# The activation and swish buffers of a fused attention and MoE kernel at other addresses relative to the weights

## The chip, the cores and the metric

One core of one Trainium2 chip. The metric is device time in microseconds for one execution; lower is better. Three runs of the kernel before took 1303.41, 1304.3 and 1307.11 us, median 1304.3 us.

## What is computed

Pooled attention, a dense swish MLP over its output, and a second MLP whose expert is chosen per token, all in float32 (N = 4608 tokens, d_model = 512):

```python
k_p = k.reshape(B, H, Sp, pool, D).mean(axis=3)          # pool = 8; v_p likewise
attn = softmax(scale * q @ k_p.T);  x = attn @ v_p       # 8 x 8 heads, 576 x 64
h = x @ w_in;  g = h * (1 / (1 + exp(-h)));  x = g @ w_out          # d_ff = 2048
...
e_idx = argmax(x @ w_gate);  do_compute = x @ w_skip > 0            # E = 8
h = maximum(x[mask] @ w1[e], 0);  y[mask] = gate_w * (h @ w2[e])    # F = 1024
out = x;  out[do_compute] += y
```

## The kernel before

**Products in three terms.** Each float32 operand of the large products is held as a high part (rounded to the matmul's float32r type) and a low part (the remainder); each product is high x high, high x low and low x high, three matmuls into one PSUM accumulator.

**The dense part** runs over 18 chunks of 256 tokens. Per chunk, attention leaves xh and xl, [128, 4, 256] words each: ScalarE copies the high part (`xh_copy`), VectorE subtracts (`xl_sub`). Then, for each of 16 blocks f of the hidden width:

- `mm1` (L320 to L328): 12 matmuls, four steps kk of three lines. L325 loads w_hi and streams xh (256 columns), L326 loads w_hi and streams xl, L327 loads w_lo and streams xh. The weight block is 128 columns, 512 bytes of a partition.
- tanh on ScalarE, `swish_t` on VectorE, then `swish_hi` (L340, ScalarE: gh) and `swish_lo` (L345, GpSimd or VectorE: gl), [128, 256] words each.
- `mm2` (L350 to L360): 6 matmuls, two token halves t of three lines. Here the activation is loaded and the weight streamed, 512 columns: L358 loads gh and streams v_hi, L359 loads gh and streams v_lo, L360 loads gl and streams v_hi.

**The order** on every engine comes from a list scheduler (`schedule`) that ranks steps by a table of costs and bonuses when the program is built; it knows how many buffers each kind has, not where they lie.

**The expert part** runs over pairs of token tiles sorted by expert: `xm1p` (L1055 to L1057) has mm1's shape with xh and xl from the same two buffers and the expert's weights in w_hi and w_lo; `xm2` (L1094 to L1096) loads hTh and hTl, which lie in v_hi, and streams weights that lie in w_hi and w_lo, 512 columns. Blocks of a single tile go through `single` (L1066 to L1068 for the first product).

**Addresses.** Pools lie one behind another in each partition's memory in the order in which they are opened, buffers of a pool behind one another. A weight block starts at its tile's start plus a multiple of 512 bytes, xh and xl blocks at their buffer's start plus a multiple of 1024, a half of gh or gl at its buffer's start or 512 behind it. So for each pair of operands the difference of their start addresses modulo 512 is one number per buffer. Start addresses modulo 512, worked out from the order and sizes of the tiles:

| tile | before | after |
|---|---|---|
| w_hi, w_lo, v_hi | 192 | 128 |
| v_lo | 384 | 448 |
| xh, first and second buffer | 256, 256 | 256, 320 |
| xl, first and second buffer | 256, 256 | 384, 416 |
| gh, three buffers | 256, 256, 256 | 416, 480, 0 |
| gl, three buffers | 256, 256, 256 | 0, 0, 0 |

Of the kernel before, what the change touches and what calls it, by code (L numbers as in the profile page):

```python
# [7 lines left out]
F32 = mybir.dt.float32  # L8
F32R = mybir.dt.float32r
BF16 = mybir.dt.bfloat16  # L10
I32 = mybir.dt.int32
# [13 lines left out]
KD = DM // 128  # L25
DFF = 2048
NF = DFF // 128
E = 8
# [3 lines left out]
NTILE = NT // 128  # L32
CH = 256
TPC = CH // 128
LAG = 3
PAIR = 256
NPX = NT // PAIR
NX = E + (NT - E) // PAIR
NXP = 28
# [13 lines left out]
def body(tc, const, q, k, v, w_in, w_out, w_skip, w_gate, w_r, w1, w2, out, x2d, lst, base, nch, nxt):  # L53
# [3 lines left out]
    with ExitStack() as ctx:  # L57
        def pool(name, bufs, **kw):
            return ctx.enter_context(tc.tile_pool(name=name, bufs=bufs, **kw))

        wp = pool("wp", 1)
        xt_p = pool("xt_p", 2)
        t_p = pool("t_p", 2)
        g_p = pool("g_p", 3)
        x2_p = pool("x2_p", 4)
        jk_p = pool("jk_p", 1)
        r_p = pool("r_p", 2)
# [7 lines left out]
        ident = const["ident"]  # L75
        triu = wp.tile([128, 128], BF16, name="triu")
        ones = wp.tile([128, 128], BF16, name="ones")
        rev = wp.tile([128, 1, E], F32, name="rev")
        ecap = wp.tile([128, 1, E], F32, name="ecap")
        tok = wp.tile([128, NTILE], F32, name="tok")  # L80
        skp = wp.tile([128, NTILE], F32, name="skp")
        wr = wp.tile([128, KD, E + 1], F32, name="wr")
# [3 lines left out]
        w4_hi = w_hi.rearrange("p f (k n) -> p f k n", n=128)  # L86
        w4_lo = w_lo.rearrange("p f (k n) -> p f k n", n=128)
        wb = wp.tile([128, (E + 1) * DM], F32, name="wb")
        pad = wp.tile([128, NTILE, 4], I32, name="pad")
        room = wp.tile([128, 6 * 512 + 6 * HP * 2 * SP], F32, name="room")  # L90
        lone = ExitStack()
        ctx.push(lone)
# [148 lines left out]
        q_t, P_t, PT_t, xh_t, xl_t = {}, {}, {}, {}, {}  # L241
# [64 lines left out]
        def x_parts(i):  # L306
            j, t = divmod(i, TPC)
            if t == 0 and j not in xh_t:
                xh_t[j] = xt_p.tile([128, KD, CH], F32R, tag="xh", name="xh")
                xl_t[j] = xt_p.tile([128, KD, CH], F32R, tag="xl", name="xl")  # L310
            return (x[j][:, :, t * 128:t * 128 + 128] for x in (xh_t, xl_t))

        def xh_copy(i):
# [24 lines left out]
            nc.vector.scalar_tensor_tensor(out=t, in0=t, scalar=1.0, in1=ps, op0=ALU.add, op1=ALU.mult)  # L338

        def swish_hi(j, f, t, ps):  # L340
            gh = g_p.tile([128, CH], F32R, tag="gh", name="gh")
            nc.scalar.copy(out=gh, in_=t)  # L342
            return j, f, t, gh

        def swish_lo(j, f, t, gh, eng=nc.vector):  # L345
            gl = g_p.tile([128, CH], F32R, tag="gl", name="gl")
            eng.tensor_tensor(out=gl, in0=t, in1=gh.bitcast(F32), op=ALU.subtract)  # L347
            g_t[j, f] = (gh, gl)

# [31 lines left out]
        sh = [128, TPC, E]  # L381

        def route_a(j):
            lg = lg_t[j]
            l = lg[:, :, 0:E]
            mx = r_p.tile([128, TPC, 1], F32, tag="rmx", name="rmx")
            m2 = r_p.tile([128, TPC, 1], F32, tag="rm2", name="rm2")
            cm = r_p.tile([128, TPC, 1], F32, tag="cm", name="cm")
            oh = r_p.tile(sh, F32, tag="oh", name="oh")
            ohb = r_p.tile(sh, BF16, tag="ohb", name="ohb")  # L390
            nc.vector.tensor_reduce(out=mx, in_=l, axis=AX.X, op=ALU.max)
            nc.vector.tensor_tensor(out=l, in0=l, in1=mx.to_broadcast(sh), op=ALU.subtract)
            nc.vector.scalar_tensor_tensor(out=oh, in0=l, scalar=0.0, in1=rev.to_broadcast(sh), op0=ALU.is_ge,
                                           op1=ALU.mult)
            nc.vector.tensor_reduce(out=m2, in_=oh, axis=AX.X, op=ALU.max)
            nc.vector.tensor_tensor(out=oh, in0=oh, in1=m2.to_broadcast(sh), op=ALU.is_equal)
            nc.vector.tensor_scalar(out=cm, in0=lg[:, :, E:E + 1], scalar1=0.0, scalar2=None, op0=ALU.is_gt)
            nc.vector.tensor_tensor(out=oh, in0=oh, in1=cm.to_broadcast(sh), op=ALU.mult)
            nc.vector.tensor_copy(out=ohb, in_=oh)
            rt[j] = (oh, ohb, cm)  # L400
# [10 lines left out]
            nc.scalar.activation(out=l, in_=l, func=ACTF.Exp)  # L411

        def route_gate(j):
            gw = r_p.tile([128, TPC, 1], F32, tag="gw", name="gw")
            nc.vector.tensor_reduce(out=gw, in_=lg_t.pop(j)[:, :, 0:E], axis=AX.X, op=ALU.add)
            nc.vector.tensor_scalar(out=gw, in0=gw, scalar1=1e-9, scalar2=None, op0=ALU.add)
            row = row_t[j] = r_p.tile([128, TPC, 4], I32, tag="row", name="row")
            nc.vector.reciprocal(out=row[:, :, 2:3].bitcast(F32), in_=gw)
            for t in range(TPC):
                i = TPC * j + t  # L420
                nc.vector.tensor_copy(out=row[:, t, 0:2], in_=tok[:, i:i + 1].to_broadcast([128, 2]))
            nc.vector.memset(row[:, :, 3:4], 0)

        def route_place(j):
            oh, ohb, cm = rt.pop(j)
            ps = rp_t.pop(j)
            ds = r_p.tile(sh, F32, tag="ds", name="ds")
            dd = r_p.tile([128, TPC, 1], F32, tag="dd", name="dd")
            du = du_t[j] = r_p.tile([128, TPC, 1], I32, tag="du", name="du")
            for t in range(TPC):  # L430
                nc.vector.tensor_tensor(out=ds[:, t], in0=ps[:, 0, t], in1=base, op=ALU.add)
                nc.vector.tensor_tensor(out=base, in0=base, in1=ps[:, 1, t], op=ALU.add)
            nc.vector.tensor_tensor(out=ds, in0=ds, in1=ecap.to_broadcast(sh), op=ALU.add)
            nc.vector.tensor_tensor(out=ds, in0=ds, in1=oh, op=ALU.mult)
            nc.vector.tensor_reduce(out=dd, in_=ds, axis=AX.X, op=ALU.add)
            i = TPC * j
            sk = skp[:, i:i + TPC].rearrange("p (t o) -> p t o", o=1)
            nc.vector.scalar_tensor_tensor(out=cm, in0=cm, scalar=0.0, in1=sk, op0=ALU.is_equal, op1=ALU.mult)
            nc.vector.tensor_tensor(out=du, in0=dd, in1=cm, op=ALU.add)
# [12 lines left out]
        def dense():  # L452
# [48 lines left out]
            def op(name, cost, fn, after=(), take=None, bonus=0.0, linger=0.0):  # L501
                bonus += bonus_of.get(name[0], {}).get(phase(*name), 0.0)
                ops[name] = (cost, fn, [a for a in after if a], take, bonus, linger)

            def put_in(key, v):
                st[key] = v
# [131 lines left out]

            tail = {(1, f): NF + f for f in range(NF - LAG, NF)}
            slot = {**tail, **{(j, f): j * NF + f for j in range(2, nch) for f in range(NF)}}  # L640
            at = {n: jf for jf, n in slot.items()}
            for j in range(nch):
                for f in range(NF):
                    n = slot.get((j, f), -1)

                    def back(name, k):
                        return n - k in at and (name, *at[n - k])
# [3 lines left out]
                       [("xl", TPC * j + t) for t in range(TPC)]  # L651
                       + [("lo", 2 * f), f > 0 and ("mm1", j, f - 1), (j, f) == (1, NF - LAG) and ("mm1", 0, NF - 1),
                          back("mm1", 1), back("sw", 2), back("mm2", LAG + 1)], [("h", ("h", j, f))])
                    op(("th", j, f), {"A": 0.27}, lambda e, j=j, f=f: put_in(("t", j, f), tanh(*st["h", j, f])),
# [164 lines left out]
        def flat(w, a, b):  # L819
            return w[:, a:b].rearrange("p f n -> p (f n)")  # L820
# [4 lines left out]
        W2h4, W2l4 = (w.rearrange("p (k n) -> p k n", n=DM) for w in (W2h, W2l))  # L825
        hTh, hTl = (flat(v_hi, a, a + 4).rearrange("p (k n) -> p k n", n=PAIR) for a in (8, 12))
        xg = [room[:, KD * F2 + a * 2 * DM:KD * F2 + (a + 1) * 2 * DM].rearrange("p (t n) -> p t n", n=DM)
# [3 lines left out]
        xT_t, own = {}, []  # L831
# [51 lines left out]
        def row_of(t):  # L883
            return t.rearrange("p e o -> p o e")

        def first_table():
# [8 lines left out]
            nc.vector.tensor_tensor(out=top, in0=key, in1=kmax.to_broadcast([1, E, 1]), op=ALU.is_equal)  # L895
            nc.vector.scalar_tensor_tensor(out=skip, in0=cnt0, scalar=float(PAIR), in1=top, op0=ALU.min, op1=ALU.mult)
            nc.vector.tensor_tensor(out=f2[:, 0:1], in0=row_of(top), in1=row_of(ie), op=ALU.mult)
# [6 lines left out]
        def table_iota():  # L904
            nc.gpsimd.iota(jt, pattern=[[0, 1], [PAIR, NPX]], base=0, channel_multiplier=0,
                           allow_small_or_imprecise_dtypes=True)
            nc.gpsimd.iota(it, pattern=[[1, NXP], [0, 1]], base=0, channel_multiplier=0,
                           allow_small_or_imprecise_dtypes=True)
            nc.gpsimd.iota(ib, pattern=[[PAIR, NXP], [0, 1]], base=0, channel_multiplier=0,
                           allow_small_or_imprecise_dtypes=True)  # L910
# [122 lines left out]

        def x_turn_hi(i, t, ps):
            if i < 2 and t == 0:
                xT_t[i] = [xt_p.tile([128, KD, PAIR], F32R, tag=tag, name=tag) for tag in ("xh", "xl")]
            nc.scalar.copy(out=xT_t[i % 2][0][:, :, t * 128:t * 128 + 128], in_=ps)

        def x_turn_lo(i, t, ps):
# [282 lines left out]
```

## Time and profile before

| | |
|---|---|
| median of three runs | 1304.3 us |
| profiled execution, its own time | 1307.36 us |
| its span, first to last instruction | 1305.6 us |
| TensorE (PE) busy | 1261.9 us, 97% |
| weight loads (PEld) busy | 1128.2 us, 86% |
| VectorE (DVE) / ScalarE (ACT) / GpSimd (POOL) busy | 809.0 / 557.4 / 458.3 us |
| mean granted TensorE clock | 0.997 of 2.4 GHz |

Busy time counts a matmul from its start to its modelled end, and matmuls overlap in the pipeline: a matmul shown with 282 ns may be followed by the next after 118 ns. So what a matmul costs when others stand behind it is read from the starts of neighbours in the timeline, and the busy share only says where TensorE is idle.

### The profile page before, as it was taken

The page shows a single profiled execution, that of the slowest core. Times are in us where ns is not written, and L with a number is a line of the kernel's source. Part 1 is how long each engine was busy: PE and PEld are TensorE (multiplying, and loading weights), DVE is VectorE, ACT ScalarE, POOL GpSimd, SP SyncE. Part 2 cuts the span into 40 slices and gives each one's busy share as a digit, 9 for nine tenths or more (in the row PEclk, how much of TensorE's full clock was granted, in tenths as well). Part 3 has the DMA queues.
Part 4 walks back from the last instruction along what each step waited for, and adds up shares of the span by engine and source line. Part 5 has one row for each costly group of instructions (what it writes and reads, how often), then busy time and mean ns, then how long its engine had stood idle before and what let it go on. Part 6 is the DMA issues. An engine that isn't in the chain of part 4 may idle for free. (4 is left out here: it accounts for less than half of the span.)

```text
span 1305.6 us, 24485 instructions
## 1 busy us (share of the span) xinstructions
PE 1261.9 (97%) x8508; PEld 1128.2 (86%) x8508; DVE 809.0 (62%) x2112; ACT 557.4 (43%) x1609; POOL 458.3 (35%) x552
## 2 busy tenths in 40 slices
PE   4899999999999999999999999999999999999986
PEld 3789889988989988889899989998998999989775
DVE  7998897576575584574675654744773222333777
ACT  4876543434434443434344444343341121223675
POOL 2312154344434333533534333332432112133654
PEclk9999999999999999999999999999999999999999
DMA  7655412101121121112110110000411111426770
GB/s 234 223 201 197 144 40 82 46 13 64 40 69 64 35 73 41 40 55 76 34 63 19 41 41 17 34 33 1 172 40 58 59 34 58 170 66 220 260 287 26
DMA packets 51152, 113.32 MB, mean 87 GB/s; under 512 B 12279, under 2 KB 13303, under 8 KB 50864
## 3 DMA queue, kind: packets, MB, share of 16 engines
q1 hardware_dynamic: 44960, 96.39, 21.7%
q0 software_dynamic: 6032, 14.97, 3.4%
q8 instruction: 80, 1.31, 0.4%
q14 instruction: 80, 0.66, 0.2%
HBM read 134.05 MB, written 26.62 MB: 123 GB/s over the span
## 5 line engine op out<-in xcount | busy, mean ns | idle before, releaser
L325 PE MATMUL psh<-xh,w_hi 128*128 128x256 f32 x1152 | 325.2, 282 | 1.0 <-DVE t L338 1.0
L326 PE MATMUL psh<-xl,w_hi 128*128 128x256 f32 x1152 | 323.1, 280 | 1.5 <-DVE xl L319 1.5
L327 PE MATMUL psh<-xh,w_lo 128*128 128x256 f32 x1152 | 322.2, 280 | 0.0
L347 POOL TENSOR_TENSOR gl<-t,gh 128x256 fp32r<-128x256 f32 x231 | 184.5, 800 | 344.8 <-ACT gh L342 230.5
L378 DVE SCALAR_TENSOR_TENSOR junk<-x,wb 128x512 bf16<-128x512 f32 x306 | 242.8, 793 | 21.7 <-ACT x L367 16.0
L338 DVE SCALAR_TENSOR_TENSOR t<-t,psh 128x256 f32<-128x256 f32 x288 | 119.5, 416 | 192.4 <-ACT t L332 190.4
L358 PE MATMUL pso<-v_hi,gh 128*128 128x512 f32 x576 | 230.3, 400 | 0.1
L332 ACT ACTIVATE t<-psh 128x256 f32<-128x256 f32 x288 | 110.8, 385 | 272.4 <-PE psh L327 248.6
L325 PEld LDWEIGHTS psh<-xh,w_hi 128*128 128x128 f32 x1152 | 216.9, 188 | 10.8 <-DVE t L338 1.5
L359 PE MATMUL pso<-v_lo,gh 128*128 128x512 f32 x576 | 226.1, 393 | 0.0
L360 PE MATMUL pso<-v_hi,gl 128*128 128x512 f32 x576 | 225.0, 391 | 0.3 <-POOL gl L347 0.3
L326 PEld LDWEIGHTS psh<-xl,w_hi 128*128 128x128 f32 x1152 | 216.9, 188 | 9.2 <-DVE xl L319 1.9
L327 PEld LDWEIGHTS psh<-xh,w_lo 128*128 128x128 f32 x1152 | 216.2, 188 | 0.0
L342 ACT CAST gh<-t 128x256 fp32r<-128x256 f32 x288 | 117.0, 408 | 150.8 <-DVE t L338 121.8
L360 PEld LDWEIGHTS pso<-v_hi,gl 128*128 128x128 f32 x576 | 108.1, 188 | 27.6 <-POOL gl L347 1.2
L358 PEld LDWEIGHTS pso<-v_hi,gh 128*128 128x128 f32 x576 | 108.0, 187 | 16.9 <-ACT gh L342 0.8
L359 PEld LDWEIGHTS pso<-v_lo,gh 128*128 128x128 f32 x576 | 108.4, 188 | 15.3
L1058 ACT ACTIVATE v_hi<-p 128x256 fp32r<-128x256 f32 x88 | 33.5, 384 | 179.0 <-PE p L1057 169.9
L1059 DVE SCALAR_TENSOR_TENSOR v_hi<-p,v_hi 128x256 fp32r<-128x256 f32 x88 | 36.9, 423 | 114.6 <-ACT v_hi L1058 103.1
L275 ACT ACTIVATE room<-pss,mx 128x72 f32<-128x72 f32 x288 | 88.1, 326 | 30.5 <-DVE mx L267 27.4
L1055 PE MATMUL p<-xh,w_hi 128*128 128x256 f32 x352 | 100.4, 285 | 0.0
L1057 PE MATMUL p<-xh,w_lo 128*128 128x256 f32 x352 | 98.3, 279 | 0.0
(189 smaller groups left out, 2118.3 us busy)
## 6 DMA issues: line engine op xcount, KB each, us to landing
more<-in_w_dram SPq DMA_DIRECT2D x72, 512.0 KB
room<-in_w_dram SPq DMA_DIRECT2D x40, 512.0 KB
wb<-in_w_dram SPq DMA_DIRECT2D x36, 512.0 KB
room<-in_k_dram SPq DMA_DIRECT2D x32, 288.0 KB
room<-in_v_dram SPq DMA_DIRECT2D x64, 144.0 KB
room<-in_q_dram SPq DMA_DIRECT2D x36, 256.0 KB
out_dram<-x SPq DMA_DIRECT2D x36, 256.0 KB
x2d<-x SPq DMA_DIRECT2D x36, 256.0 KB
```

The costliest lines, as they stand in the source:

```text
L325: nc.tensor.matmul(out=ps, lhsT=w4_hi[:, f, kk], rhs=xh[:, kk], start=(kk == 0), stop=False)
L326: nc.tensor.matmul(out=ps, lhsT=w4_hi[:, f, kk], rhs=xl[:, kk], start=False, stop=False)
L327: nc.tensor.matmul(out=ps, lhsT=w4_lo[:, f, kk], rhs=xh[:, kk], start=False, stop=(kk == KD - 1))
L332: nc.scalar.activation(out=t, in_=ps, func=ACTF.Tanh, scale=0.5)
L338: nc.vector.scalar_tensor_tensor(out=t, in0=t, scalar=1.0, in1=ps, op0=ALU.add, op1=ALU.mult)
L342: nc.scalar.copy(out=gh, in_=t)
L347: eng.tensor_tensor(out=gl, in0=t, in1=gh.bitcast(F32), op=ALU.subtract)
L358: nc.tensor.matmul(out=ps, lhsT=gh[:, ts], rhs=v_hi[:, f], start=(f == 0), stop=False)
L359: nc.tensor.matmul(out=ps, lhsT=gh[:, ts], rhs=v_lo[:, f], start=False, stop=False)
L360: nc.tensor.matmul(out=ps, lhsT=gl[:, ts], rhs=v_hi[:, f], start=False, stop=(f == NF - 1))
L378: nc.vector.scalar_tensor_tensor(out=junk, in0=x2_t[i], scalar=1.0, in1=wb[:, e * DM:e * DM + DM], op0=ALU.mult, op1=ALU.mult, accum_out=l ...
L1055: nc.tensor.matmul(out=ps, lhsT=W1h4[:, kk, m], rhs=xh[:, kk], start=(kk == 0), stop=False)
```

## The change

The two xh, two xl, three gh and three gl buffers get a pool of their own each, opened in the order of two tables; a number other than 0 in a table puts an unused tile of that many bytes ahead of the buffer. `rev`, `ecap` and `pad`, small tiles of the routing, move from the weights' pool to places between these buffers. Five small route tiles (rmx, rm2, gw, ds, dd) get one buffer instead of two. Chunk j uses buffer j % 2 of xh and xl as before, and the gh and gl buffers are used in turn as before. The instructions and their order on each engine stay the same.

```diff
+SPOTS_X = (("rev", 0), ("xh0", 64), ("xh1", 64), ("pad", 0), ("xl0", 0), ("xl1", 32))
+SPOTS_G = (("gh0", 0), ("gh1", 64), ("gh2", 32), ("gl0", 0), ("gl1", 0), ("gl2", 0))
...
-        xt_p = pool("xt_p", 2)
+        sep = [0]
+
+        def own_pool(name, gap):
+            if gap:
+                sep[0] += 1
+                pool(f"sep{sep[0]}", 1).tile([128, gap // 4], F32, name="sep")
+            return pool(name, 1)
+
+        x_p = {}
+        for n, gap in SPOTS_X:
+            if n == "rev":
+                x_p[n] = pool("rev_p", 1)
+            elif n == "pad":
+                x_p[n] = pool("pad_p", 1)
+            else:
+                x_p[n] = own_pool("p" + n, gap)
         t_p = pool("t_p", 2)
-        g_p = pool("g_p", 3)
+        g_ps = {n: own_pool("p" + n, gap) for n, gap in SPOTS_G}
+        turn = {"x": [], "gh": 0, "gl": 0}
+
+        def x_tiles(side):
+            for part in ("xh", "xl"):
+                n = f"{part}{side}"
+                yield x_p[n].tile([128, KD, CH], F32R, tag=n, name=part)
+
+        def g_tile(part):
+            n = turn[part]
+            turn[part] = n + 1
+            return g_ps[f"{part}{n % 3}"].tile([128, CH], F32R, tag=f"{part}{n % 3}", name=part)
...
-        rev = wp.tile([128, 1, E], F32, name="rev")
-        ecap = wp.tile([128, 1, E], F32, name="ecap")
...
-        pad = wp.tile([128, NTILE, 4], I32, name="pad")
+        pad = x_p["pad"].tile([128, NTILE, 4], I32, name="pad")
+        rev = x_p["rev"].tile([128, 1, E], F32, name="rev")
+        ecap = x_p["rev"].tile([128, 1, E], F32, name="ecap")
...
-                xh_t[j] = xt_p.tile([128, KD, CH], F32R, tag="xh", name="xh")
-                xl_t[j] = xt_p.tile([128, KD, CH], F32R, tag="xl", name="xl")
+                xh_t[j], xl_t[j] = x_tiles(j % 2)
...
-            gh = g_p.tile([128, CH], F32R, tag="gh", name="gh")
+            gh = g_tile("gh")
...
-            gl = g_p.tile([128, CH], F32R, tag="gl", name="gl")
+            gl = g_tile("gl")
...
-            ds = r_p.tile(sh, F32, tag="ds", name="ds")
-            dd = r_p.tile([128, TPC, 1], F32, tag="dd", name="dd")
+            ds = r_p.tile(sh, F32, tag="ds", name="ds", bufs=1)
+            dd = r_p.tile([128, TPC, 1], F32, tag="dd", name="dd", bufs=1)
...
-                xT_t[i] = [xt_p.tile([128, KD, PAIR], F32R, tag=tag, name=tag) for tag in ("xh", "xl")]
+                xT_t[i] = list(x_tiles(i))
```

## Rows read from the trace of the kernel before

**Rows 1.** The page: span, busy time of each engine, granted clock in tenths by slice.

```profile
span 1305.6 us, 24485 instructions
PE 1261.9 (97%) x8508; PEld 1128.2 (86%) x8508; DVE 809.0 (62%) x2112; ACT 557.4 (43%) x1609; POOL 458.3 (35%) x552
...
PEclk9999999999999999999999999999999999999999
```

**Rows 2.** Busy us (x instructions) by stretch: PE, PEld, DVE, ACT, POOL; clock, DMA share, GB/s.

```profile
0.00:60.00 60.00, 37.25 (x208) 30.91 (x208) 51.33 (x101) 38.17 (x116) 19.41 (x37) 1.00 0.68 225
60.00:200.00 140.00, 137.19 (x962) 122.77 (x961) 127.58 (x313) 85.23 (x256) 33.95 (x50) 1.00 0.43 146
200.00:1000.00 800.00, 798.09 (x5585) 718.57 (x5584) 491.94 (x1526) 327.88 (x1058) 307.00 (x396) 1.00 0.15 51
1000.00:1140.00 140.00, 140.00 (x927) 128.61 (x927) 37.95 (x74) 26.04 (x63) 24.46 (x24) 1.00 0.22 70
1140.00:1306.00 166.00, 149.40 (x835) 127.34 (x834) 100.23 (x102) 80.12 (x119) 73.52 (x45) 0.98 0.50 174
```

**Rows 3.** Groups by form on PE: shapes, xcount | busy us, mean ns | idle before.

```profile
L325 PE MATMUL psh<-xh,w_hi 128*128 128x256 f32 x1152 | 325.2, 282 | 1.0 <-DVE t L338 1.0
...
L327 PE MATMUL psh<-xh,w_lo 128*128 128x256 f32 x1152 | 322.2, 280 | 0.0
L358 PE MATMUL pso<-v_hi,gh 128*128 128x512 f32 x576 | 230.3, 400 | 0.1
L359 PE MATMUL pso<-v_lo,gh 128*128 128x512 f32 x576 | 226.1, 393 | 0.0
L360 PE MATMUL pso<-v_hi,gl 128*128 128x512 f32 x576 | 225.0, 391 | 0.3 <-POOL gl L347 0.3
L1055 PE MATMUL p<-xh,w_hi 128*128 128x256 f32 x352 | 100.4, 285 | 0.0
...
L1094 PE MATMUL py<-w_hi,v_hi 128*128 128x512 f32 x80 | 31.2, 390 | 0.0
```

**Rows 4.** Timeline of PE, mm2 then mm1: start us, us, line, operands.

```profile
399.75 0.40 PE L358 MATMUL pso<-v_hi,gh 128*128 128x512 f32 x1
399.99 0.39 PE L359 MATMUL pso<-v_lo,gh 128*128 128x512 f32 x1
400.22 0.40 PE L360 MATMUL pso<-v_hi,gl 128*128 128x512 f32 x1
400.45 0.40 PE L358 MATMUL pso<-v_hi,gh 128*128 128x512 f32 x1
400.69 0.39 PE L359 MATMUL pso<-v_lo,gh 128*128 128x512 f32 x1
400.92 0.39 PE L360 MATMUL pso<-v_hi,gl 128*128 128x512 f32 x1
401.15 0.28 PE L325 MATMUL psh<-xh,w_hi 128*128 128x256 f32 x1
...
403.97 0.40 PE L358 MATMUL pso<-v_hi,gh 128*128 128x512 f32 x1
```

**Rows 5.** Timeline of PEld, the weight loads, in the same stretch.

```profile
399.75 0.19 PEld L359 LDWEIGHTS pso<-v_lo,gh 128*128 128x128 f32 x1
...
401.15 0.19 PEld L326 LDWEIGHTS psh<-xl,w_hi 128*128 128x128 f32 x1
```

**Rows 6.** Timeline of PE, xm2 of one pair: its first matmul and what follows its 48.

```profile
1118.03 0.39 PE L1094 MATMUL py<-w_hi,v_hi 128*128 128x512 f32 x1
...
1128.93 0.28 PE L1055 MATMUL p<-xh,w_hi 128*128 128x256 f32 x1
```

**Rows 7.** Timeline of PE, the sixteen short matmuls of the last router sums.

```profile
967.16 1.85 PE L1122 MATMUL psl<-wr,x2T 128*128 128x9 f32 x16
968.86 0.36 PE L1055 MATMUL p<-xh,w_hi 128*128 128x256 f32 x1
```

**Rows 8.** Busy us (x instructions) of L325 alone between 60 and 200 us.

```profile
60.00:200.00 140.00, 47.92 (x170) 1.00 0.43 146
```

More of the change, by code (lines that the diff above doesn't have):

```diff
@@ L385, in route_a @@
             l = lg[:, :, 0:E]
-            mx = r_p.tile([128, TPC, 1], F32, tag="rmx", name="rmx")
-            m2 = r_p.tile([128, TPC, 1], F32, tag="rm2", name="rm2")
+            mx = r_p.tile([128, TPC, 1], F32, tag="rmx", name="rmx", bufs=1)
+            m2 = r_p.tile([128, TPC, 1], F32, tag="rm2", name="rm2", bufs=1)
             cm = r_p.tile([128, TPC, 1], F32, tag="cm", name="cm")
@@ L413, in route_gate @@
         def route_gate(j):
-            gw = r_p.tile([128, TPC, 1], F32, tag="gw", name="gw")
+            gw = r_p.tile([128, TPC, 1], F32, tag="gw", name="gw", bufs=1)
             nc.vector.tensor_reduce(out=gw, in_=lg_t.pop(j)[:, :, 0:E], axis=AX.X, op=ALU.add)
```

## The prediction

> **What bounds the kernel now.** I read the page first [rows 1]: TensorE is busy for 1261.9 of 1305.6 us (97%), VectorE for 62%, and the granted clock stands at its upper level, 2.4 GHz, in every slice. The table by stretches [rows 2] shows where the rest is: between 200 and 1000 us TensorE is idle for 1.9 us, between 1000 and 1140 us for none. So in those 940 us nothing but TensorE sets the time; it is idle for 22.8 us before 60 us and for 16.6 us after 1140 us. Between 60 and 200 us VectorE is busy for 127.6 of 140 us, so a faster TensorE would gain less there.
>
> The groups by form [rows 3] give the counts. mm1 issues its three lines together, 1152 matmuls of 256 columns on each, and xm1p its three, 352 on each: 4512 instructions of one shape. mm2 has three lines of 576 (512 columns); in xm2 the row of py stands for its shape. A busy matmul is not a matmul at its peak, so I take steps from start to start [rows 4]: from 401.15 to 403.97 us stand 24 matmuls of mm1, 117.5 ns each; the six of mm2 ahead of them take 1.40 us, 233.3 ns each. In xm2 [rows 6] 48 matmuls of 512 columns take 10.90 us, 227.1 ns each. The same work at the same clock: 6 ns apart.
>
> What differs is where the operands lie. Each matmul streams one operand while the stationary one of the next is loaded: the load of L359 starts in the same hundredth of a microsecond as the matmul of L358 [rows 4, 5]. For such a pair I take the start of the activation side less that of the weight side, modulo 512. Before, every pair of mm1 and xm1p has 64; in mm2 L358 and L360 (v_hi streams, gh is loaded) have 64, L359 (v_lo streams, gl is loaded) has 384; xm2 has 0. The mean durations [rows 3] follow in part: at 0, 390 ns (py); at 384, 393; at 64, 400 and 391, in the mean 395.5.
>
> **The change, part by part.** No instruction is added, removed or moved: every engine has the same rows in the same order. What moves is addresses. In mm1 and xm1p the pair goes from 64 to 128 or 192 (xh) and 256 or 288 (xl). In mm2 L358 and L360 go from 64 to 288, 352 or 384, in turn; L359 goes from 384 to 64; xm2 stays at 0.
>
> 1. mm1 and xm1p. No row has 256 columns at the new distances, so I bound the step. Below: 256 more columns cost 227.1 - 117.5 = 109.6 ns [rows 4, 6], so a step holds 7.9 ns that its columns don't need; without them, 4512 x 7.9 ns = 35.6 us less. The load alone doesn't stop this: the 16 short matmuls of L1122, each behind a load of 128 columns, step by (968.86 - 967.16)/16 = 106 ns [rows 7]. Above: the mean at 64 is 5.5 ns over that at 0; if the new distances cost that more than now, 4512 x 5.5 = 24.8 us. The nearest row to the new distances is L359's, at 384, which is 128 the other way round: 2.5 ns under the mean at 64. There is one weight load to a matmul in either shape, so I take the same 2.5 ns per matmul: 4512 x 2.5 = 11.3 us less.
> 2. mm2. L358 and L360 (1152 instructions) go from the mean at 64 to about 384: 1152 x 2.5 = 2.9 us less. L359 (576) goes the other way: 1.4 us more. Net 1.4 us less; at best all six step as in xm2, 1728 x (233.3 - 227.1) = 10.7 us less; at worst L358 and L360 keep theirs and L359 reaches L358's 400, 576 x 7 = 4.0 us more.
> 3. xm2 at nothing: its distance stays. The one-tile blocks at the end (L1066 to L1068) at nothing: they stand in the last stretch, where TensorE is idle for 16.6 us anyway [rows 2], and are few.
> 4. Five small route tiles lose their second buffer. Each is written and read by VectorE alone, in its own order, so no wait comes of it: nothing. Moving pad, rev and ecap, and the separators, costs no instruction.
>
> Of this the matmuls of mm1 between 60 and 200 us, three lines of 170 [rows 8], may lose their 510 x 2.5 ns = 1.3 us to VectorE; I leave that to the range. Sum: -11.3 - 1.4 = **-12.7 us**. The profiled execution took 1307.4 us and would take 1294.7; it lies 3.1 us above the median of the three runs, 1304.3, from which the sum gives 1291.6.
>
> Here a page speaks against the change. The rows show a matmul step that differs by 6 ns between mm2 and xm2 [rows 4, 6]. The Trainium skill, "TensorE: Matmul & The Clock Gate", Part 2, step 1, says that TensorE reads the streaming operand and the weights through two independent ports, and that loading the next weights takes no read bandwidth from the running matmul. By that the sum would be 0 and not -12.7 us. By that rule steps of one shape should be alike wherever the operands lie, and these traces show two that aren't.
>
> **The rivals.**
> - *Nothing to gain.* If the 117.5 ns of mm1 are the stream's and the load's own (106 ns for a load [rows 7] plus a hand-over), no distance matters for 4512 of the instructions, and mm2's two shifts nearly cancel: 1304. For it: L325 and L327, which load from different weight tiles, agree to 2 ns, and L360, at 64, takes 391, hardly more than xm2's 390 [rows 3], so the address may not be what tells L358 from L360. Against it: mm2 and xm2 differ. The page of the Trainium skill named above, "TensorE: Matmul & The Clock Gate", would give this case.
> - *The distances are worse.* The load takes 106 ns for its 512 bytes [rows 7], in which the stream of mm1 reads its 1024 bytes; so the stream gains 512 bytes on the load and passes it once, modulo 512. Where depends on the distance: at 0 at the very ends of the load (xm2, 390 ns), at 64 in mm1 after seven eighths of it; in L359 at three quarters (393 ns), in L358 at one eighth (400 ns). If a passing in the midst costs more than one near the end, the change moves all 4512 to between seven sixteenths and three quarters: with L359's excess over xm2, 3 ns, 4512 x 3 = 13.5 us more, 1318. It decides from the point at which xl0 and xl1, the middle ones, make L326 step longer than L325 and L327. For it: 0 is the best distance in the trace and the change leaves it further behind. Against it: L360 sits at the place of L358 and pays 1 ns.
> - *It doesn't do what it says*: the addresses follow from the order and sizes of the tiles, so I give that no chance of its own.
>
> **How the numbers follow.** A fewer-stalls case gets 0.48, nothing to gain 0.22, worse distances 0.30. About 0.3% (3.9 us) is what a measurement of this kernel can tell from no change; the first case lies beyond it from 0.9 ns per matmul of mm1 on, the third likewise, so the chances are those of the cases. The predicted time is the first case's, 1292 us (the sum, rounded up). The ends of the unknown costs are 1304.3 - 35.6 - 10.7 = 1258 and 1304.3 + 24.8 + 4.0 = 1333; both ask that every buffer hit its extreme, and the distances differ from buffer to buffer. 1268 to 1320 leaves out about one in ten on either side and holds the rivals' 1304 and 1318. The first case's own range is 1268 to 1300.
>
> **What would show it.** Right: steps of mm1 near 115 ns instead of 117.5 between mm2 and mm2, other for chunks with even and odd number (xh0, xh1) if the distance is what counts; L358 down from 400 towards 393, L359 up; xm2 still at 227; TensorE's busy time down by about the same 13 us, VectorE's, ScalarE's and GpSimd's as before. Wrong: 117.5 unchanged in both buffers (nothing to gain), or steps over 120 ns, first in L326 (worse distances). A gain outside TensorE's own steps would refute the whole argument.

## The result, and the profile after

The change made the kernel slower: 1312.5 us against 1305.0, ratio 1.0052 with a 95% interval of 1.0038 to 1.0066. One of the changed kernel's 13 runs, 1393.5 us at a mean granted clock of 0.854, counts in its median but not in the ratio. The prediction was 1292 us, faster. The time lies inside the stated range, but the sign is wrong.

The page of the changed kernel's profile (span, then busy time, share of the span and instructions by engine; its own time is 1316.6 us):

```profile
span 1314.9 us, 24486 instructions
PE 1271.3 (97%) x8508; PEld 1137.1 (86%) x8508; DVE 808.0 (61%) x2112; ACT 558.2 (42%) x1609; POOL 457.7 (35%) x552
```

TensorE's busy time rose by 9.4 us, from 1261.9 [rows 1] to 1271.3, and the span by 9.3 us. VectorE, ScalarE and GpSimd are within 1.0 us of before. The table by stretches (busy us and, in brackets, instructions of PE, PEld, DVE, ACT and POOL; clock; DMA) says what TensorE did with the time:

```profile
200.00:1000.00 800.00, 798.60 (x5536) 718.15 (x5535) 489.34 (x1522) 326.08 (x1053) 306.80 (x396) 1.00 0.15 50
1000.00:1140.00 140.00, 140.00 (x923) 128.74 (x922) 37.86 (x74) 25.70 (x61) 24.47 (x24) 1.00 0.19 62
```

Between 200 and 1000 us TensorE is idle for 1.4 us, not longer than before [rows 2], at the same clock, and starts 5536 matmuls there instead of 5585. So no wait has come in: the matmuls themselves follow each other more slowly. The groups by form (matrix, shapes, count | busy us, mean ns | idle before) show which; L353 to L355 are the old L325 to L327, L386 to L388 the old L358 to L360, L1083 the old L1055:

```profile
L353 PE MATMUL psh<-xh,w_hi 128*128 128x256 f32 x1152 | 329.7, 286 | 0.8 <-DVE t L366 0.7
L355 PE MATMUL psh<-xh,w_lo 128*128 128x256 f32 x1152 | 326.7, 284 | 0.0
L354 PE MATMUL psh<-xl,w_hi 128*128 128x256 f32 x1152 | 325.0, 282 | 1.5 <-DVE xl L347 1.5
L386 PE MATMUL pso<-v_hi,gh 128*128 128x512 f32 x576 | 229.7, 399 | 0.2
L388 PE MATMUL pso<-v_hi,gl 128*128 128x512 f32 x576 | 227.8, 395 | 0.0
L387 PE MATMUL pso<-v_lo,gh 128*128 128x512 f32 x576 | 226.8, 394 | 0.0
L1083 PE MATMUL p<-xh,w_hi 128*128 128x256 f32 x352 | 101.3, 288 | 0.0
```

Against [rows 3] both lines of mm1 that stream xh last 4 ns longer (286 and 284 for 282 and 280). xl's line lasts 2 ns longer, 282 for the 280 of before:

```profile
L326 PE MATMUL psh<-xl,w_hi 128*128 128x256 f32 x1152 | 323.1, 280 | 1.5 <-DVE xl L319 1.5
```

In mm2 the line that loads gl has 395 for 391, the others are within 1 ns.

The loss, summed from each matmul's start to the next one's over the whole profiled execution, after less before: mm1 422.3 - 416.9 = 5.4 us, mm2 406.6 - 405.1 = 1.5, xm1p 127.4 - 126.3 = 1.1, the one-tile products 37.8 - 36.2 = 1.6, xm2 -0.3, all other matmuls 0.3; together 9.6 us. With the first matmul starting 0.2 us earlier, that is the 9.3 us of the spans within the rounding. So 8.0 us of it are steps of mm1, mm2 and xm1p. The 1.6 us of the one-tile products are waits: their four steps over 0.6 us, which wait for transfers into `own` and `room` or for w_lo, took 10.3 us, 8.4 before, and the other 116 took 27.6 us, 27.8 before. The longest of these waits, before and after (L1059 is the old L1031):

```profile
1260.37 1.06 PE L1031 MATMUL pst<-ident,own 128*128 128x128 f32 x8 [2.49 <-DMA own<-x2d,room]
1268.71 1.94 PE L1059 MATMUL pst<-ident,own 128*128 128x128 f32 x8 [3.95 <-DMA own<-x2d,room]
```

### The profile page after: what moved, and what is told of

It reads as the page before. It is cut to its first block, busy times and chain, and to the rows that moved or that the text cites. A ratio compares the mean times of both kernels' runs of the same rounds, so it can differ in the third digit from the quotient of the medians.

```text
span 1314.9 us, 24486 instructions
## 1 busy us (share of the span) xinstructions
PE 1271.3 (97%) x8508; PEld 1137.1 (86%) x8508; DVE 808.0 (61%) x2112; ACT 558.2 (42%) x1609; POOL 457.7 (35%) x552
## 5 line engine op out<-in xcount | busy, mean ns | idle before, releaser
L353 PE MATMUL psh<-xh,w_hi 128*128 128x256 f32 x1152 | 329.7, 286 | 0.8 <-DVE t L366 0.7
L355 PE MATMUL psh<-xh,w_lo 128*128 128x256 f32 x1152 | 326.7, 284 | 0.0
L360 ACT ACTIVATE t<-psh 128x256 f32<-128x256 f32 x288 | 110.7, 384 | 282.3 <-PE psh L355 264.6
L386 PE MATMUL pso<-v_hi,gh 128*128 128x512 f32 x576 | 229.7, 399 | 0.2
L353 PEld LDWEIGHTS psh<-xh,w_hi 128*128 128x128 f32 x1152 | 219.0, 190 | 10.4 <-DVE t L366 1.3
L388 PE MATMUL pso<-v_hi,gl 128*128 128x512 f32 x576 | 227.8, 395 | 0.0
L355 PEld LDWEIGHTS psh<-xh,w_lo 128*128 128x128 f32 x1152 | 217.7, 189 | 0.0
L388 PEld LDWEIGHTS pso<-v_hi,gl 128*128 128x128 f32 x576 | 108.3, 188 | 26.2 <-POOL gl L375 0.6
L386 PEld LDWEIGHTS pso<-v_hi,gh 128*128 128x128 f32 x576 | 108.4, 188 | 16.9 <-ACT gh L370 0.8
L1083 PE MATMUL p<-xh,w_hi 128*128 128x256 f32 x352 | 101.3, 288 | 0.0
```

The source lines that it names most:

```text
L353: nc.tensor.matmul(out=ps, lhsT=w4_hi[:, f, kk], rhs=xh[:, kk], start=(kk == 0), stop=False)
L355: nc.tensor.matmul(out=ps, lhsT=w4_lo[:, f, kk], rhs=xh[:, kk], start=False, stop=(kk == KD - 1))
L360: nc.scalar.activation(out=t, in_=ps, func=ACTF.Tanh, scale=0.5)
L386: nc.tensor.matmul(out=ps, lhsT=gh[:, ts], rhs=v_hi[:, f], start=(f == 0), stop=False)
L388: nc.tensor.matmul(out=ps, lhsT=gl[:, ts], rhs=v_hi[:, f], start=False, stop=(f == NF - 1))
L1083: nc.tensor.matmul(out=ps, lhsT=W1h4[:, kk, m], rhs=xh[:, kk], start=(kk == 0), stop=False)
```

## The experiments

All kernels use one list in place of the two tables. A number is a gap in bytes ahead of the next buffer, `rev` and `pad` stay with the weights where the list has none of them, and GAP_V is a gap ahead of v_lo:

```diff
-SPOTS_X = (("rev", 0), ("xh0", 64), ("xh1", 64), ("pad", 0), ("xl0", 0), ("xl1", 32))
-SPOTS_G = (("gh0", 0), ("gh1", 64), ("gh2", 32), ("gl0", 0), ("gl1", 0), ("gl2", 0))
+SPOTS = ("pad", "xh0", "xh1", "xl0", "xl1", "gh0", "gh1", "gh2", "gl0", "gl1", "gl2")
+GAP_V = 192
...
-        for n, gap in SPOTS_X:
+        for n in SPOTS:
+            if isinstance(n, int):
+                gap = n
+            else:
+                x_p[n] = own_pool("p" + n, gap)
+                gap = 0
```

That list is the first experiment's. In all of them the instructions and their order are those of the kernel before. The diffs below are against it; where none gives GAP_V, nothing stands ahead of v_lo. Distances below are from w_hi, modulo 512. "Eleven" is the time from the first to the last of the twelve matmuls of one mm1, the mean over those in which no step exceeds 130 ns (252 to 254 of 288), for first and second buffer; mm1 and mm2 are the sums over all 3456 and 1728 of them, from start to next start. Both come from one profiled execution of each kernel, and a row without a ratio rests on one execution altogether. Three pairs of rows have the same distances (before and e1, the change and e13, e11 and e14); their sums differ by 0.2 to 1.2 us in mm1 and by 0.1 to 0.3 in mm2, so smaller differences say nothing.

| run | xh | xl | gh / gl / v_lo | eleven, ns | mm1, us | mm2, us | ratio to before, interval |
|---|---|---|---|---|---|---|---|
| before | 64 | 64 | 64 / 64 / 192 | 1295, 1295 | 416.9 | 405.1 | |
| the change | 128, 192 | 256, 288 | 288, 352, 384 / 384 / 320 | 1314, 1311 | 422.3 | 406.6 | 1.0052 (1.0038 to 1.0066) |
| e1_control | 64 | 64 | 64 / 64 / 192 | 1296, 1296 | 417.1 | 404.8 | 0.9982 (0.9971 to 0.9994) |
| e2_x_alone | 128, 192 | 256, 288 | 64 / 96 / 224 | 1305, 1308 | 419.9 | 407.0 | 1.0036 (1.0022 to 1.0049) |
| e3_gh_alone | 64 | 64 | 288, 352, 384 / 384 / 320 | 1296, 1296 | 417.1 | 406.3 | 1.0009 (0.9993 to 1.0025) |
| e4_all_zero | 0 | 0 | 0 / 0 / 0 | 1314, 1315 | 423.0 | 403.2 | 1.0043 (1.0028 to 1.0058) |
| e5_x_32_96 | 32, 96 | 32, 96 | 128 / 128 / 64 | 1288, 1318 | 419.9 | 406.0 | |
| e6_x_128_192 | 128, 192 | 128, 192 | 256 / 256 / 192 | 1304, 1287 | 416.8 | 404.3 | |
| e7_x_256_320 | 256, 320 | 256, 320 | 320 / 320 / 256 | 1303, 1296 | 418.1 | 409.1 | |
| e8_x_384_416 | 384, 416 | 384, 416 | 416 / 416 / 352 | 1308, 1301 | 419.2 | 406.3 | |
| e9_x32_g0 | 32 | 32 | 0 / 0 / 0 | 1286, 1285 | 414.5 | 402.6 | 0.9963 (0.9951 to 0.9975) |
| e10_xh_xl_apart | 64, 192 | 192, 64 | 64 / 64 / 192 | 1292, 1296 | 417.4 | 403.9 | 0.9984 (0.9972 to 0.9996) |
| e11_xl_alone | 64 | 256, 288 | 64 / 96 / 224 | 1307, 1294 | 419.2 | 408.6 | 1.0039 (1.0024 to 1.0054) |
| e12_xh_alone | 128, 192 | 64 | 64 / 96 / 224 | 1292, 1296 | 416.9 | 408.2 | 1.0021 (1.0006 to 1.0035) |
| e13_xh_by_512 | 128, 192 | 256, 288 | as the change | 1314, 1311 | 421.6 | 406.7 | 1.0042 (1.0027 to 1.0057) |
| e14_all_by_512 | 64 | 256, 288 | as e11 | 1307, 1294 | 418.0 | 408.5 | |
| e15_x_224_288 | 224, 288 | 224, 288 | 64 / 64 / 224 | 1301, 1286 | 416.7 | 405.8 | |
| e16_gl_v_lo_32 | 64 | 64 | 64 / 96 / 224 | 1295, 1295 | 416.4 | 410.2 | |

**Is it the distances at all?** e1 keeps pools, single route buffers and spacers, and puts every distance back.

> Everything of the change but the distances: pools of their own, one buffer for the five route tiles, and x, gh and gl back at 64 from the weights, v_lo at 192. If the distances make the time, mm1 steps by 117.7 ns and mm2's six take 1387 ns as before, and the time is that of the kernel before, 1304 to 1307 us. If the rest of the change makes it (route tiles, separate pools, other bases), 1311 to 1313 us with the steps of before.

Measured: 0.9982, the steps of before, and in the table by stretches 5589 matmuls where before had 5585:

```profile
200.00:1000.00 800.00, 798.18 (x5589) 718.94 (x5588) 492.18 (x1527) 328.01 (x1058) 306.68 (x396) 1.00 0.15 51
```

So the loss is in the distances; the other parts of the change cost nothing. With every distance of before e1 still lies 0.18% under it: about that much two kernels differ without any help of the distances. Where larger ratios exist, the steps follow them: mm1, mm2 and xm1p together took 8.0 us more in the change (6.8 us by its ratio), 6.3 more in e4 (5.6) and 5.8 less in e9 (4.8).

**Which distances?** e2 moves x alone, e3 gh, gl and v_lo alone; their lists, in this order:

```diff
-SPOTS = ("pad", "xh0", "xh1", "xl0", "xl1", "gh0", "gh1", "gh2", "gl0", "gl1", "gl2")
-GAP_V = 192
+SPOTS = (64, "gh0", "gh1", "gh2", 32, "gl0", "gl1", "gl2", 32, "xh0", 64, "xh1", 64, "xl0", 32, "xl1")
+SPOTS = ("pad", "xh0", "xh1", "xl0", "xl1", "rev", 160, "gh0", 64, "gh1", 32, "gh2", "gl0", "gl1", "gl2")
```

> x at the new distances 128, 192, 256, 288; gh back at 64, and gl 384 ahead of v_lo as before. If distances act pair by pair, mm1's steps are those of the changed kernel (358 ns per three for the first buffers, 360 for the second, against 353 before: 5.4 us over 3456 matmuls, 1.1 us in xm1p, 1.6 us in the one-tile blocks) and mm2's six stay at 1387 ns: 1305 + 8 = 1313 us. If the change's loss comes of gh or of the rest, mm1 stays at 353 and the time at 1305.

> gh, gl and v_lo at the new distances, all x back at 64. If distances act pair by pair, mm1 has 353 ns per three as before, mm2's six take 1399, 1395 and 1385 ns with the three gh buffers as in the changed kernel, in the mean 1.5 us in all: 1305 + 1.5 = 1306.5 us. If gh is what costs, 1312.

Measured: e3 costs nothing that can be told from no change, and mm1 has its old steps beside the changed mm2. e2 costs 0.36%. But its mm1 gains back almost half (419.9, not 422.3 us) although every x distance is the change's, and its mm2 is 1.9 us slower than before although gh kept its distance to v_hi and gl to v_lo. Neither theory had foreseen that.

**Is the price that of a pair?** e4 puts every distance at 0:

```diff
-SPOTS = ("pad", "xh0", "xh1", "xl0", "xl1", "gh0", "gh1", "gh2", "gl0", "gl1", "gl2")
-GAP_V = 192
+SPOTS = ("xh0", "xh1", "xl0", "xl1", "gh0", "gh1", "gh2", "gl0", "gl1", "gl2")
+GAP_V = 64
```

> x, gh, gl and v_lo all at distance 0 from the weights. If the distance of the pair sets the step, mm2's six step as xm2 does, 6 x 227 = 1362 ns instead of 1387, and mm1 at 117.2 ns: 288 x 25 ns + 3456 x 0.5 ns = 9 us less than before, 1296 us, faster than both. If xm2 is quick for another reason (fewer engines at work beside it, its tiles), mm2 stays at 1387 and the time at 1305.

Measured: 1.0043, slower, against my theory. mm1 took 423.0 us instead of 416.9. Its groups:

```profile
L352 PE MATMUL psh<-xh,w_hi 128*128 128x256 f32 x1152 | 329.1, 286 | 1.0 <-DVE t L365 0.9
L353 PE MATMUL psh<-xl,w_hi 128*128 128x256 f32 x1152 | 327.0, 284 | 1.5 <-DVE xl L346 1.5
L354 PE MATMUL psh<-xh,w_lo 128*128 128x256 f32 x1152 | 326.8, 284 | 0.0
```

The lines of xh last 4 ns longer than before [rows 3], that of xl too (280 before). And six matmuls of mm2 at 0 do not step like xm2; these take, from the first row to the second,

```profile
405.11 0.40 PE L385 MATMUL pso<-v_hi,gh 128*128 128x512 f32 x1
...
406.50 0.28 PE L352 MATMUL psh<-xh,w_hi 128*128 128x256 f32 x1
```

1.39 us, 231.7 ns each, against 227.1 for xm2's forty-eight [rows 6]. So distance 0 alone doesn't make a six of mm2 quick. But 55 of the 214 runs of mm2 are longer than six, and there it does. A run of 18, its first, seventh and thirteenth matmul and what follows it, in the kernel before and in e4:

```profile
413.79 0.40 PE L358 MATMUL pso<-v_hi,gh 128*128 128x512 f32 x1
...
415.18 0.39 PE L358 MATMUL pso<-v_hi,gh 128*128 128x512 f32 x1
...
416.56 0.39 PE L358 MATMUL pso<-v_hi,gh 128*128 128x512 f32 x1
...
417.95 0.28 PE L325 MATMUL psh<-xh,w_hi 128*128 128x256 f32 x1
```

```profile
415.00 0.40 PE L385 MATMUL pso<-v_hi,gh 128*128 128x512 f32 x1
...
416.38 0.39 PE L385 MATMUL pso<-v_hi,gh 128*128 128x512 f32 x1
...
417.74 0.39 PE L385 MATMUL pso<-v_hi,gh 128*128 128x512 f32 x1
...
419.10 0.28 PE L352 MATMUL psh<-xh,w_hi 128*128 128x256 f32 x1
```

Before, each six takes 1.38 to 1.39 us. In e4 the first takes 1.39 us, the other two 1.36, 226.7 ns each, as in xm2. Over all sixes without a wait, the first of a run takes 231.3 ns per matmul before and 231.2 in e4, a later one 230.8 before and 226.7 in e4 and 226.9 in e9. xm2 starts no quicker; its seventh matmul, in the kernel before, is

```profile
1119.41 0.39 PE L1094 MATMUL py<-w_hi,v_hi 128*128 128x512 f32 x1
```

so its first six take 230 ns each and the other 42 226.7. xm2 was quick for both reasons together: its distance, and runs long enough to get past the first six.

**The sweep.** e5 to e8 give xh and xl of one buffer the same distance, two distances in each kernel, with gh and gl behind them:

```diff
-SPOTS = ("pad", "xh0", "xh1", "xl0", "xl1", "gh0", "gh1", "gh2", "gl0", "gl1", "gl2")
-GAP_V = 192
+SPOTS = (32, "xh0", "xl0", 64, "xh1", "xl1", 32, "gh0", "gh1", "gh2", "gl0", "gl1", "gl2")
+SPOTS = ("pad", "rev", "xh0", "xl0", 64, "xh1", "xl1", 64, "gh0", "gh1", "gh2", "gl0", "gl1", "gl2")
+SPOTS = ("pad", "rev", 128, "xh0", "xl0", 64, "xh1", "xl1", "gh0", "gh1", "gh2", "gl0", "gl1", "gl2")
+SPOTS = ("pad", "rev", 256, "xh0", "xl0", 32, "xh1", "xl1", "gh0", "gh1", "gh2", "gl0", "gl1", "gl2")
```

> xh and xl of the first buffer at 32, of the second at 96 (gh, gl at 128). Known for uniform x: 117.7 ns at 64, 120 at 0. Smooth in the distance (best near 64): 118 to 119 at both, mm1 in all 1 to 4 us over before. A period of 128 bytes (64 is good, 0 is bad): 119 at both. Best distance elsewhere: one of them under 117.

> x of the first buffer at 128, of the second at 192 (gh, gl at 256). Smooth: 120 to 121 at both. Period 128: 120 at 128, 117.7 at 192. Place where the stream passes the load: 119 and 120.

> x of the first buffer at 256, of the second at 320 (gh, gl at 320). Smooth: 121 and more at both, mm1 over 12 us above before. Period 128: 120 at 256, 117.7 at 320. Place of the passing: 121, then falling.

> x of the first buffer at 384, of the second at 416 (gh, gl at 416). Smooth: 120 to 121. Period 128: 120 at 384, 119 at 416. Place of the passing: about 119 falling to 118.

Measured, ns per eleven by distance: 1314 at 0 (e4), 1288 at 32, 1295 at 64, 1318 at 96, 1304 at 128, 1287 at 192, 1303 at 256, 1296 at 320, 1308 at 384, 1301 at 416. None of the shapes I had written fits. It is neither smooth nor of period 128, and it doesn't rise towards the middle. Distances 256 apart come out alike at 64 and 320 and nearly so at 128 and 384, but not at 0 and 256. The change's four distances, each shared by xh and xl, would cost 1304, 1287 and 1303 (and, by e15, 1286 at 288), in the mean 1295: what 64 costs.

**Do distances mix?** e10 gives xh and xl two distances that are good when shared. e11 and e12 then take the two halves of the change's x one at a time, xl alone and xh alone:

```diff
-SPOTS = ("pad", "xh0", "xh1", "xl0", "xl1", "gh0", "gh1", "gh2", "gl0", "gl1", "gl2")
-GAP_V = 192
+SPOTS = ("pad", "gh0", "gh1", "gh2", "gl0", "gl1", "gl2", "xh0", "xl1", 128, "xh1", "xl0")
+GAP_V = 64
+SPOTS = ("pad", "gh0", "gh1", "gh2", "xh0", "xh1", 32, "gl0", "gl1", "gl2", 160, "xl0", 32, "xl1")
+SPOTS = ("pad", "gh0", "gh1", "gh2", "xl0", "xl1", 32, "gl0", "gl1", "gl2", 32, "xh0", 64, "xh1")
+GAP_V = 96
```

> Two distances that are good when xh and xl share them, 64 and 192, given to xh and xl of one buffer: 64 and 192 in the first, 192 and 64 in the second; gh, gl, v_lo as before. If each pair costs by its own distance, mm1 takes 1288 to 1296 ns per eleven in both buffers, 415 us in all, and the time is 1303 to 1305 us. If a distance that changes from one matmul to the next costs of itself, 1305 to 1315 ns per eleven, mm1 420 to 422 us and the time 1310 to 1313 us.

> Of the change's x only xl: 256 and 288, with xh of both buffers back at 64; gh at 64, gl 384 ahead of v_lo, as in the run with all x moved. If the slow steps belong to xh's own distances (the matmuls that stream xh step by 120 ns in the changed kernel, those that stream xl by 117.5), mm1 is at 417 us as before and the time at 1305 to 1307 us. If xl's place slows the xh matmuls next to it, 1305 to 1315 ns per eleven, mm1 420 to 422 us and 1310 us.

> Of the change's x only xh: 128 and 192, with xl of both buffers back at 64; gh, gl, v_lo as in the run before this one. If the slow steps belong to xh's own distances, the first buffer takes 1314 and the second 1311 ns per eleven as in the changed kernel, mm1 422 us and the time 1310 us. By the runs with one distance for xh and xl (1305 at 128, 1288 at 192, 1295 at 64) and costs that add, 1302 and 1290, mm1 416 us and the time 1304 us. If xl's place is what costs, also 416 to 417.

Measured: e10's mm1 stays at 417.4 us, so a mixture doesn't cost of itself. e12's mm1 stays at 416.9, so xh's distances alone don't cost, and the reading that I had put first for both runs falls. e11's goes to 419.2, all in the first buffer. The change's 5.4 us is neither of the halves nor their sum. e2 shows it with the same gh, gl and v_lo as e11 and e12: its second buffer takes 1308 ns per eleven, where each half alone takes 1294 or 1296. e11 also shows single matmuls, not all, that are slow (timeline of PE, one mm1 of the first buffer, L350 to L352):

```profile
403.07 0.28 PE L350 MATMUL psh<-xh,w_hi 128*128 128x256 f32 x1
403.19 0.29 PE L351 MATMUL psh<-xl,w_hi 128*128 128x256 f32 x1
403.31 0.28 PE L352 MATMUL psh<-xh,w_lo 128*128 128x256 f32 x1
403.43 0.28 PE L350 MATMUL psh<-xh,w_hi 128*128 128x256 f32 x1
403.55 0.28 PE L351 MATMUL psh<-xl,w_hi 128*128 128x256 f32 x1
403.67 0.28 PE L352 MATMUL psh<-xh,w_lo 128*128 128x256 f32 x1
```

From L351 to L352 pass 0.12 to 0.13 us at the first kk and 0.12 at the second; in the trace's nanoseconds 128 and 117, and so in turn, slow at kk = 0 and 2, in 100 of the 123 mm1 of this buffer without a wait. Operands at one distance modulo 512 cost 11 ns more or less. Two explanations were left: distances count modulo 1024 (an odd kk differs by 512 there), or the matmuls before matter.

**Modulo 512, or more?** e13 is the change with `pad` ahead of xh0 and `rev` between xh1 and xl0: xh moves by 512 against everything else. e14 is e11 with x, gh, gl and v_lo moved by 512 against the weights. e15 gives the first buffer 224 and the second 288; e16 is e1 with 32 bytes between gh and gl. In this order:

```diff
-SPOTS = ("pad", "xh0", "xh1", "xl0", "xl1", "gh0", "gh1", "gh2", "gl0", "gl1", "gl2")
-GAP_V = 192
+SPOTS = ("pad", 64, "xh0", 64, "xh1", "rev", "xl0", 32, "xl1", "gh0", 64, "gh1", 32, "gh2", "gl0", "gl1", "gl2")
+SPOTS = (64, "gh0", "gh1", "gh2", "xh0", "xh1", 32, "gl0", "gl1", "gl2", 160, "xl0", 32, "xl1")
+SPOTS = ("pad", "gh0", "gh1", "gh2", "gl0", "gl1", "gl2", "rev", 96, "xh0", "xl0", 64, "xh1", "xl1")
+SPOTS = ("pad", "xh0", "xh1", "xl0", "xl1", "gh0", "gh1", "gh2", 32, "gl0", "gl1", "gl2")
+GAP_V = 192
```

> The changed kernel with both xh buffers 512 bytes nearer, by the order of the tiles: every distance modulo 512 is the change's. If only the distance modulo 512 counts, mm1 takes 1314 and 1311 ns per eleven as in the change, 422 us, and the time is 1312 us. If the distance modulo 1024 counts, other numbers: with xh and xl in the same half, as in the run with all x moved, about 1305 and 1307, mm1 420 us, 1309 us.

> The run with xl alone, with x, gh, gl and v_lo all 512 bytes further from the weights, distances modulo 512 unchanged. Modulo 512 alone: the two steps of 127 ns stay at the xl matmuls of kk = 0 and 2 of the first buffer. Modulo 1024: they go to kk = 1 and 3, and mm1's sum stays about 419 us.

> xh and xl together at 224 in the first buffer and 288 in the second, gh at 64. If 288 is bad in itself, 1305 to 1315 ns per eleven in the second buffer; if it is the mixture of xh and xl that costs, 1290 to 1300 in both.

> x and gh at 64 as before; gl at 96 and v_lo at 224, both 32 further than before, so that the load of gl keeps its distance to the stream of v_lo. If pairs of load and stream are all, mm2 is at 405 us as before. If it matters where the next stream or load lies against the last one (v_hi to v_lo, gh to gl), mm2 is at 407 to 408.6 us as in the three runs that had gl at 96.

Measured: e13 has the change's mm1 to the nanosecond, 1314 and 1311 per eleven. In e14 the slow steps are where they were in e11, at kk = 0 and 2:

```profile
401.64 0.28 PE L350 MATMUL psh<-xh,w_hi 128*128 128x256 f32 x1
401.76 0.29 PE L351 MATMUL psh<-xl,w_hi 128*128 128x256 f32 x1
401.89 0.28 PE L352 MATMUL psh<-xh,w_lo 128*128 128x256 f32 x1
402.00 0.28 PE L350 MATMUL psh<-xh,w_hi 128*128 128x256 f32 x1
402.12 0.28 PE L351 MATMUL psh<-xl,w_hi 128*128 128x256 f32 x1
402.24 0.28 PE L352 MATMUL psh<-xh,w_lo 128*128 128x256 f32 x1
```

So a shift by 512 changes nothing, and the step is not a matter of kk's address. In e14 every tile also lies 64 bytes further on modulo 512 (the weights start at 256, in e11 at 192): in these two it is the distances that count, not the places. e15's 288, shared, is as good as 32 (1286), while 192 and 288 mixed took 1311 in the change. e16 kept the distance of every loaded tile to the tile that streams meanwhile, gh to v_hi and gl to v_lo, and mm2 still rose from 405.1 to 410.2 us in its one execution, all three lines lasting 2 to 4 ns longer than before [rows 3]:

```profile
L385 PE MATMUL pso<-v_hi,gh 128*128 128x512 f32 x576 | 231.3, 402 | 0.3 <-ACT gh L369 0.2
L386 PE MATMUL pso<-v_lo,gh 128*128 128x512 f32 x576 | 228.0, 396 | 0.0
L387 PE MATMUL pso<-v_hi,gl 128*128 128x512 f32 x576 | 227.6, 395 | 0.3 <-POOL gl L374 0.3
```

**The matmuls before matter.** That is seen best within the changed kernel itself. Twenty-four matmuls of mm1 on blocks f = 5 and 6, second buffer, from the first row to the second, in two chunks of the same execution:

```profile
320.66 0.28 PE L353 MATMUL psh<-xh,w_hi 128*128 128x256 f32 x1
...
323.49 0.40 PE L386 MATMUL pso<-v_hi,gh 128*128 128x512 f32 x1
```

```profile
423.44 0.28 PE L353 MATMUL psh<-xh,w_hi 128*128 128x256 f32 x1
...
426.31 0.39 PE L386 MATMUL pso<-v_hi,gh 128*128 128x512 f32 x1
```

The first 24 take 2.83 us, the second 2.87: the same lines, weight blocks, x buffers, distances and clock. In nanoseconds the first run repeats 119, 119, 115 (353 per three), the second 124, 116, 120 (360). In the kernel before, 252 of the 253 mm1 without a wait repeat 353 or 354 (the mean over their last nine steps). In the change 110 of 122 in the first buffer and 87 of 131 in the second repeat 360; in e13, 111 of 123 and 87 of 131; in e9, 235 of 253 repeat 350. So the distances modulo 512 decide which repeating patterns there are. What decides among them is not the address of the weights or of x, as the two stretches above show. I take it to be what the run of matmuls enters with, since 51 of the change's 61 pairs of mm1 that follow each other without a break or a wait keep their pattern from the first to the second; no run tests this by itself, or sets it apart from what the other engines do meanwhile. It would explain why the halves of the change don't add up, and why mm1 with the same x differs between e2 and the change, whose mm2 ahead of it differ. Where x lies at a shared 64, a slower mm2 ahead changes nothing: mm1 keeps its 353 in e3 and e16.

**A version that beats both.** e9 takes 32 for x and 0 for the rest:

```diff
-SPOTS = ("pad", "xh0", "xh1", "xl0", "xl1", "gh0", "gh1", "gh2", "gl0", "gl1", "gl2")
-GAP_V = 192
+SPOTS = ("gh0", "gh1", "gh2", "gl0", "gl1", "gl2", 32, "xh0", "xh1", "xl0", "xl1")
+GAP_V = 32
```

> All x at 32, gh, gl and v_lo at 0: for each shape the best of the distances looked at so far. If a step belongs to the distance, mm1 takes 1285 ns per eleven steps in both buffers (1295.5 before), 3.3 us less over 3456 matmuls, xm1p 1 us less, and mm2's six 1378 ns (1387 before), 2 us less: 1299 us, some 0.5% under before. If the good steps at 32 hung on the other buffer's 96 or on the gh beside it, 1305 or more.

Measured: 1301.9 us, ratio 0.9963 (0.9951 to 0.9975), faster than before and 0.9% faster than the change (0.9963/1.0052 = 0.991). The steps of mm1 give 2.4 us, of mm2 2.5, of xm1p 0.9. Against e1 (0.9982) the ratio leaves only 0.2% to the distances; the 5.8 us of steps are the firmer evidence. Its groups and its stretch from 200 to 1000 us:

```profile
L352 PE MATMUL psh<-xh,w_hi 128*128 128x256 f32 x1152 | 325.9, 283 | 1.1 <-DVE t L365 1.0
L353 PE MATMUL psh<-xl,w_hi 128*128 128x256 f32 x1152 | 322.1, 280 | 1.5 <-DVE xl L346 1.5
L354 PE MATMUL psh<-xh,w_lo 128*128 128x256 f32 x1152 | 322.0, 280 | 0.0
L385 PE MATMUL pso<-v_hi,gh 128*128 128x512 f32 x576 | 229.0, 398 | 0.3 <-ACT gh L369 0.2
L386 PE MATMUL pso<-v_lo,gh 128*128 128x512 f32 x576 | 226.3, 393 | 0.0
L387 PE MATMUL pso<-v_hi,gl 128*128 128x512 f32 x576 | 224.8, 390 | 0.3 <-POOL gl L374 0.2
```

```profile
200.00:1000.00 800.00, 797.90 (x5609) 719.90 (x5608) 493.22 (x1526) 329.84 (x1061) 307.75 (x396) 1.00 0.15 51
```

5609 matmuls in the stretch, 24 more than before.

## Why the prediction was wrong

**What bounds the kernel** was right: TensorE has next to no idle time to give between 200 and 1140 us, and the 8.0 us of longer steps arrived in the span.

**"What differs is where the operands lie"**, read from mm2 against xm2, was half right. e4 put mm2 at xm2's distance, and the sixes that follow other sixes went from 230.8 to 226.7 ns per matmul; the first six of each run stayed at 231, and 159 of mm2's 214 runs are six long. How long a run of one shape lasts I had in front of me [rows 4, 6] and didn't weigh. The change itself put no mm2 at 0.

**Step 1, mm1 and xm1p**, is the step that failed. I took 2.5 ns per matmul off, from "the nearest row to the new distances", L359's at 384. Measured: 5.4 us/3456 = 1.6 ns more in mm1 and 1.1 us/1056 = 1.0 ns more in xm1p. A price of one line of mm2 cannot be carried to mm1, because a step isn't priced by its own pair: 384 shared by xh and xl cost mm1 1308 per eleven, more than the 1295 of 64. Nor was the price right for mm2. I read it from mean durations, whose ends are modelled. By the starts of the 237 mm2 without a wait in the kernel before, the step from L359 (at 384) takes 231.7 ns, those from L358 and L360 (at 64) 234.2 and 227.7, in the mean 230.9: 384 was 0.8 ns dearer than 64, not 2.5 cheaper. The bounds of the step held (109.6 to 123 ns). **Step 2, mm2**: 1.4 us less forecast, 1.5 more in the profile, 1.2 more in e3, whose time can't be told from no change.

**Steps 3 and 4** held where they can be tested: xm2 moved by 0.3 us, and e1 shows that the route tiles and spacers cost nothing. The one-tile products, put at nothing, took 1.6 us more in the profile, all of it in waits; over all kernels here they range from 30.8 to 38.8 us, so that is not put down to the change.

**The rivals.** "The distances are worse" had the sign, at 1318 for 1312.5, but not the mechanism: it wanted xl's line slowest, at the middle distances; that line is the quickest of the three, and 256 and 288 shared cost 1303 and 1286. "Nothing to gain" is out. The Trainium skill's page "TensorE: Matmul & The Clock Gate", Part 2, step 1, says that loading weights takes no read bandwidth from the running matmul. Read as I had read it, that where the operands lie cannot matter, it doesn't agree with these traces: moving tiles by some bytes took mm1 from 414.5 us (e9) to 423.0 (e4), both at the upper clock and with TensorE idle for about 2 us between 200 and 1000 us. The measurement decides. Whether the stream and the load share a read, or what else they share, no run here shows.

**The chances** leaned on one-row evidence for the sign. With rows for 0, 64 and 384 only, from a shape other than mm1's, there was no ground for 0.48 on one side.

## What to carry to other kernels

Where TensorE is back to back, sum its steps from start to start before and after any change of the layout, even one that only adds a small tile: here the best and the worst layout lie 0.9% apart with the same instructions. Try a few distances of a matmul loop's operands from the weights modulo a weight block, and keep the one whose steps sum to the least; don't infer one shape's price from another shape's row. And keep experiments at whole kernels: halves of a layout don't add up.

## What the runs showed that I had not expected

- The time of a run of matmuls can repeat in patterns of three: nearly all mm1 without a wait took 353 ns per three at 64 (before), 360 at 0 (e4) and 350 at 32 (e9), at the upper clock; other layouts mix several values. The same lines on the same weight blocks and x buffers fell into 353 and 360 within one execution.
- A move by 512 bytes counts for nothing, one by 32 does: xh moved by 512 left mm1 at 1314 and 1311 ns per eleven, while 32 bytes more (64 to 96) took a shared x from 1295 to 1318.
- More than the pair matters: gl and v_lo moved on together by 32 bytes, with each pair's distance kept, cost mm2 5.1 us in the one execution of e16. Whether it is gl's place beside gh or v_lo's beside v_hi, no run here shows.
